# Gated recurrence and four experts on one core: row sums, loads and copies of the attention units moved, and the newer form of unit begun one unit earlier

## The chip, the cores and the metric

The kernel runs on one core of a Trainium2 chip, as one launch. The metric is the device time of the run in microseconds (us). The core's engines are PE (matrix products), DVE, ACT and POOL (elementwise work), and SP, which here only issues DMAs; PE's weight loads are shown apart as PEld. Each engine works through its own queue in order and waits on semaphores that other engines or DMAs raise.

## What is computed

The first part is a gated linear recurrence over 768 steps for 4 batches of 8 heads with 48 columns; the second sends its output through four small two-layer networks ("experts") and adds their results with normalised weights.

```python
# q, k, v, alpha: (4, 8, 768, 48)
for t in range(S):
    state = alpha[:, :, t, :, None] * state + np.einsum('bhd,bhe->bhde', k[:, :, t], v[:, :, t])
    y[:, :, t] = np.einsum('bhd,bhde->bhe', q[:, :, t], state)
x = y.transpose(0, 2, 1, 3).reshape(B * S, H * D)            # (3072, 384)
...
p = domain_probs / (domain_probs.sum(-1, keepdims=True) + 1e-09)
for e in range(E):                                           # E = 4, w1 384 x 1024, w2 1024 x 384
    h = np.maximum(x @ w1[e], 0.0)
    out += p[:, e:e + 1] * (h @ w2[e])
```

## The kernel before

**Units.** The sequence is cut into 6 chunks of 128 tokens (`cb`); one chunk of one batch `b` is a unit, so there are 24 units (0 to 23), dealt chunk by chunk. They form groups of 2, 4, 4, 4, 4, 4 and 2 units. A unit's result is a slice of `xT`, the input of the experts for its group. The attention of a group runs beneath the experts' work of the group before it; in the start-up the first two units run alone and beneath the first expert.

**The experts.** `up(gi, e, fc)` (L962) makes one of 8 slices of a hidden layer: after group 0 nine matmuls of 128x512 into a PSUM tile `one` (three products of high and low parts, L995), ACT's relu into the high part of `hT` (L1003), and later, one slice behind, DVE's low part (`hidden_rest`, L1035), which reads `one` again and so gives the PSUM buffer back. `one` and the sums `ops` of `down` (L1038, matmuls L1083) share four PSUM buffers, tag "g". `add_up` (L1107 and L1109) weights the sums. Weights are split once into high and low parts (L261 to L264, `kept`) and later loaded from there (`w<-kept`, L234).

**A unit in the older form** is `attention(u)` (L718). It turns alpha, k and q into columns (PE transposes `tp`, L295, or DVE for units from `in_runs` = 6 on), then doubles the span of tokens that a block covers in seven levels (m = 1, 2, 4 to 64). Level `li` has a copy of query halves into a tile `qb` (`copy_q`, L781, two copies of 64 partitions on ACT), `next_q` (L788 on DVE and the decay product L790 on POOL) and `next_k` (a copy of key halves, L799, and L800 on DVE). The decay tile `AT` is multiplied in place, so each level's query and key products read what POOL's product of the level before wrote. Levels 0 to 5 give score products on PE (`sc`, L807), of which DVE takes the wanted parts into `near` (L817); level 6 gives `far` (L863). After that come the copies into `lat`, the output products `yps` (L902), the keys turned by PE (`tp`, four transposes, copied by ACT at L735 for alpha and in `turn_keys` for keys), the state products `sps`, and the state update (L941). `sps` and `tp` share the PSUM tag "w" with two buffers.

**A unit in the newer form** is `in_order(u)` (L497), taken from `in_fours` = 8 on. Levels 0 and 1 are replaced by products of four neighbouring tokens: q is loaded by fours into two large tiles (eight DMAs, L183) and three shifted rows of alpha into `ra` (L186); POOL multiplies them (L517 twice, then L520 and L521 for each tile), DVE sums the rows into `dot` (L531), and a later step writes those sums into `near`. The two levels still advance queries, keys and decays, but have no copies into `qb`, no score products and no takes. Levels 2 to 6 stay (`copy_q` L551, `next_q` L557 and L559, `next_k` L568 and L571, score products L604). The keys are turned through DRAM: DVE transposes blocks into a tile that POOL stores in `over` (L644), and four DMAs of SP load them back over `AT` (`AT<-over`, L656) for the state products (L696). These units run two at a time, overlapped: the tail of unit u-1 runs inside unit u.

**The order.** Each unit is a generator, and each `yield` ends a step. `deal()` (L1129) gives every step a time on a clock that `advance()` (L1185) moves by the estimated cost of each slice of experts' work; when the clock passes a step's time, the step's instructions are put into the queues of their engines, behind what is there. The tables `BEATS`, `HEAD_EARLY`, `HEAD`, `HEAD_FIRST`, `HEAD_SECOND` and `REST` (L137 to L142) hold the times as shares of a unit; `HEAD_FIRST` and `HEAD_SECOND` are those of the first two units of the newer form. The second unit is `attention(1)`, whose steps are set by hand in the start-up. `load(u, names)` (L155) issues a unit's loads on SP; it is called from steps of the unit before, and the loads of q by fours write the tiles that the unit before sums up, so they come behind its row sums. `load(u + 2, "v")` is in an older unit's last step. Large tiles for the newer form are popped one after the other out of twelve tiles (`raws`) that hold unsplit weights in the beginning.

Of the kernel before, what the change touches and what calls it, by code (L numbers as in the profile page):

```python
# [16 lines left out]
AX = mybir.AxisListType  # L17
# [3 lines left out]
def kernel(  # L21
# [11 lines left out]
    nc = tc.nc  # L33

    B, H, S, D = q.shape
# [5 lines left out]
    QUAD = 32  # L41
# [13 lines left out]
    n = np.arange(QUAD)[None, :]  # L55
# [4 lines left out]
    t = np.arange(HALF)[None, :]  # L60
# [30 lines left out]
    half = B // 2  # L91
# [10 lines left out]
    NTOK = P // QUAD  # L102
# [5 lines left out]
    fours = {}  # L108
# [32 lines left out]
    HEAD_SECOND = [0.02, 0.06, 0.1, 0.13, 0.16, 0.2, 0.25, 0.31, 0.37, 0.45, 0.52, 0.61, 0.66]  # L141
    REST = [0.05, 0.17, 0.3, 0.42, 0.58]  # L142
    in_runs = half + B
    in_fours = half + 2 * B - 2
    MARGIN = 6.0
    waiting = deque()
    clock = 0.0
# [7 lines left out]
    def load(u, names):  # L155
        if u >= len(units):
            return
        cb, b = units[u]
        for nm in names:
            src = srcs[nm][b, :, cb * P:(cb + 1) * P, :].rearrange("h s d -> s h d")  # L160
            if u == in_fours and nm == "q":
                nc.gpsimd.memset(row_a, 1.0)
            if u == in_runs and nm != "v":
                nc.gpsimd.memset(runs_of[nm][:, :, RUN - HD // 4:], 0.0)
            for g in range(P // QUAD if u >= in_runs and nm != "v" else 0):
                i, tail = divmod(g, 2)
                off, n = (QUAD, RUN - HD // 4) if tail else (0, RUN)
                runs = srcs[nm][b].rearrange("(a i) s d -> i a (s d)", i=2)[
                    i, :, cb * P * D:(cb + 1) * P * D].rearrange("a (t n) -> t a n", t=QUAD)
                nc.sync.dma_start(out=runs_of[nm][QUAD * g:QUAD * (g + 1), :, :n],  # L170
                                  in_=runs[:, :, off:off + n])
            if u >= in_runs and nm == "a":
                continue
            if u < in_fours or nm != "q":
                nc.sync.dma_start(out=raw(u, nm)[:, :, :D], in_=src)  # L175
                continue
            by_four = lambda t: t[b, :, cb * P:(cb + 1) * P].rearrange("h (t f) d -> t h (f d)", f=FOUR)
            if u == in_fours:
                four_tiles.extend(whole_raw(keep=True).rearrange("p (h f d) -> p h f d", f=FOUR, d=D) for _ in range(2))
            fours[u] = four_tiles  # L180
            for i, t in enumerate(fours[u]):
                for j in range(FOUR):
                    nc.sync.dma_start(out=t[j::FOUR].rearrange("p h f d -> p h (f d)"),  # L183
                                      in_=by_four(q)[:, H // 2 * i:H // 2 * (i + 1)])
            for j in range(FOUR - 1):
                nc.sync.dma_start(out=row_a[j::FOUR].rearrange("p h f d -> p h (f d)")[:, :, D * j:],  # L186
                                  in_=by_four(alpha)[:, :, D * (j + 1):])
# [309 lines left out]
    def in_order(u):  # L497
        cb, b = units[u]
        k = u - in_fours
        keep = cb < NCB - 1  # L500
# [6 lines left out]
        AT, QT = AT_of[k % 3], QT_of[k % 3]  # L507
# [10 lines left out]
        for i, t in enumerate(fours[u]):  # L518
            some = slice(H // 2 * i, H // 2 * (i + 1))
# [6 lines left out]
        turn("k", KT)  # L526
        yield
        dots = hid.tile([P, H, FOUR], F32, name="dot", bufs=1)
        for i, t in enumerate(fours.pop(u)):
            some = slice(H // 2 * i, H // 2 * (i + 1))  # L530
            nc.vector.reduce_sum(out=dots[:, some], in_=t, axis=AX.X)  # L531
            yield
        load(u + 1, "k")
        turn("q", QT)
        nc.vector.tensor_mul(QT, QT, AT)
        yield
        load(u + 1, "q")

        decs = [AT]
        KTs = [KT]  # L540
# [33 lines left out]
        for li in range(2):  # L574
            next_q(li)
            next_k(li)
            yield
        if k == 0:
            fifth = whole_raw(keep=True)[:, :NP * P].rearrange("p (a i n) -> p a i n", i=2, n=HALF)
            nc.gpsimd.memset(fifth, 0.0)  # L580
            free.append(fifth)
# [54 lines left out]
        if keep:  # L636
            next_k(6)
            if not quads:
# [3 lines left out]
                                in_=KTs[-1].rearrange("x a (t n) -> x a t n", n=QUAD))  # L642
            over = dram.tile([P, NTOK, NP * QUAD], F32, name="over", bufs=2)
            nc.gpsimd.dma_start(out=over, in_=by_quad.rearrange("x t a c -> x t (a c)"))  # L644
        yield
        parts = lat.rearrange("p (r s i) c -> p r s i c", s=2, i=2)
        for s in range(2):
            rows = slice(HALF * s, HALF * (s + 1))
# [3 lines left out]
            rows = slice(HALF * s, HALF * (s + 1))  # L652
            nc.scalar.copy(out=lat[rows, :, rows], in_=near[rows])
        yield
        for t in range(NTOK if keep else 0):
            nc.sync.dma_start(out=AT[QUAD * t:QUAD * (t + 1)],  # L656
                              in_=over.rearrange("(g r) t n -> t r g n", r=QUAD)[t])

        st = sts[b]
        flat_st = st.rearrange("p a i d -> p a (i d)")  # L660
# [57 lines left out]
    def attention(u):  # L718
        cb, b = units[u]
# [27 lines left out]

        own = rk[:, :, :D]
        own_late = u == 1
        copy_k = nc.gpsimd.tensor_copy if u == 1 else nc.scalar.copy  # L750
        if not own_late:
            nc.gpsimd.tensor_mul(own, rq[:, :, :D], own)
        yield
# [20 lines left out]
        def copy_q(li):  # L774
            m = LEVELS[li]
            qv = halves(QT, m)[:, :, :, 1, :]
            qb = free.popleft()
            qbs[li] = qb
            for i in range(2):
                rows = slice(HD * i, HD * (i + 1))  # L780
                nc.scalar.copy(out=qb[rows, :, i, :].rearrange("p a (b r) -> p a b r", r=m),  # L781
                               in_=qv[rows])

        def next_q(li):
            m = LEVELS[li]
# [7 lines left out]
        def next_k(li):  # L793
            m = LEVELS[li]
            old = new = halves(KTs[li], m)
            if li + 1 < len(LEVELS):
                KTs.append(keys())
                new = halves(KTs[-1], m)
                copy_k(out=new[:, :, :, 1, :], in_=old[:, :, :, 1, :])  # L799
            nc.vector.tensor_mul(new[:, :, :, 0, :], old[:, :, :, 0, :],  # L800
                                 spread(halved(decs[li])[:, :, :, 1], m))

# [326 lines left out]
    def deal():  # L1129

        wanted = [0.0]
        ends = [0.0, 0.0]
        events = []
        times = []
        t = 0.0
        for (gi, e), after in zip(tasks, tasks[1:]):
            part = 1 - 1 / len(groups[0]) if gi == e == 0 else 1
            t += (cost(0, gi, e) * FCH + cost(1, gi, e) * len(groups[gi])) * part  # L1140
            if after[1] == 0:
                wanted.append(t)

        for gis in [*([gi] for gi in range(1, LAST - 1)), [LAST - 1, LAST]]:
            gi, due = gis[0], wanted[gis[-1]] - MARGIN
            n = sum(len(groups[i]) for i in gis)
            first = wanted[gi - 1] - MARGIN * (2 < gi < LAST - 1) if gi > 1 else 0.0
            space = (due - first) / (n if gi > 1 else (n + 1) / 2)
            if gi == 1:
                space /= 2  # L1150
            for k in range(n):
                u = sum(map(len, groups[:gi])) + k
                end = due - (n - 1 - k) * space
                begin = max(end - 2 * space, ends[-2])
                ends.append(end)
                if u >= in_fours:
                    run = in_order(u)
                    burst, lead = ends[-2], ends[-2] - ends[-3]
                    span = end - burst
                    if u < in_fours + 2:  # L1160
                        times.append([burst - lead * (1 - f) for f in (HEAD_FIRST, HEAD_SECOND)[u - in_fours]])
                    else:
                        times.append([ends[-3] - (ends[-3] - ends[-4]) * (1 - f) for f in HEAD_EARLY])
                        times[-1] += [burst - lead * (1 - f) for f in HEAD]
                    times[-1] += [burst] + [burst + span * f for f in REST] + [end] * (u == len(units) - 1)
                    events += [(time, u, run) for time in times[-1]]
                    continue
                run = attention(u)
                beats = [0.0, *BEATS]
                due_at = {-1: begin, **{j: begin + (end - begin) * beats[j + 1] for j in (7, 11, 16)}}  # L1170

                marks = sorted(due_at)
                times.append([])
                for lo, hi in zip(marks, marks[1:]):
                    times[-1] += [due_at[hi] if j == hi else
                                  due_at[lo] + (due_at[hi] - due_at[lo]) * (beats[j + 1] - beats[lo + 1])
                                  / (beats[hi + 1] - beats[lo + 1]) for j in range(lo + 1, hi + 1)]

                for j, ahead in ((6, 13), (12, 15)):
                    if times[:-1]:  # L1180
                        times[-1][j] = max(times[-1][j], times[-2][ahead] + 0.5)
                events += [(time, u, run) for time in times[-1]]
        return sorted(events, key=lambda x: x[:2])

# [88 lines left out]
```

## Time and profile before

| | |
|---|---|
| median of 3 runs | 962.15 us (961.38 to 962.58) |
| the profiled execution | 961.24 us |
| its span (first to last instruction) | 959.5 us |
| busy time of PE, DVE, ACT, POOL | 948.1, 523.8, 376.4, 283.1 us |
| granted TensorE clock | 1.0 |
| DMA moved | 188.09 MB, mean 196 GB/s |
| largest groups on PE: L1083 / L995 | 376.0 us (x2112) / 361.4 us (x1656) |

The busy time of an engine is the time in which it had an instruction at work; the rest of the span is idle time, and the profile names for each idle stretch the instruction or DMA that ended it. In rows of the timeline the columns are the start and the length in us, the engine, the line and operation, the tiles written and read, the shape, how many records the row holds, and in brackets the idle time before it and its releaser. A row of L807 or L604 counts two records for a product. Lines are those of the kernel before; in the changed kernel most stand one to six lines higher or lower.

### The profile page before, as it was taken

What the parts mean: (1) busy time and instruction counts of PE and PEld (TensorE: products, weight loads), DVE (VectorE), ACT (ScalarE), POOL (GpSimd) and SP (SyncE); (2) the same over time, 40 slices, a digit from 0 to 9 for tenths busy, and PEclk for the clock granted to TensorE, in tenths of its full rate; (3) what the DMA queues carried; (4) which work ended last, traced back from release to release, by engine and by line L of the source; (5) the groups of instructions that cost most, each with busy time, mean ns of one, the idle gap of its engine ahead of it and who ended that gap; (6) DMA issues with size and microseconds to landing.
All of it is one profiled execution on the core that took longest, in us unless ns stands there. A gap on an engine that the chain in (4) does not pass through costs nothing.

```text
span 959.5 us, 21105 instructions
## 1 busy us (share of the span) xinstructions
PE 948.1 (99%) x8456; PEld 854.2 (89%) x8456; DVE 523.8 (55%) x971; ACT 376.4 (39%) x819; POOL 283.1 (30%) x397
## 2 busy tenths in 40 slices
PE   9999999999999999999999999999999999999998
PEld 7788778898998988989989989889899899999997
DVE  5667767577666665755646647647674312221222
ACT  5687756445154243242441441544234212021111
POOL 3332332444453441542533425424441000000000
PEclk9999999999999999999999999999999999999999
DMA  7999758697866687746686864678870006070701
GB/s 175 281 327 283 234 149 260 230 345 239 279 222 203 179 301 250 207 169 177 188 287 205 269 204 126 196 252 216 272 229 25 20 4 260 1 264 1 262 18 33
DMA packets 171270, 188.09 MB, mean 196 GB/s; under 512 B 83436, under 2 KB 151404, under 8 KB 171172
## 3 DMA queue, kind: packets, MB, share of 16 engines
q1 hardware_dynamic: 163748, 153.74, 53.2%
q0 software_dynamic: 6976, 32.64, 8.8%
q8 instruction: 67, 1.10, 0.5%
q10 hardware_dynamic: 448, 0.36, 0.2%
q14 instruction: 31, 0.25, 0.1%
HBM read 153.67 MB, written 33.03 MB: 195 GB/s over the span
## 4 chain that ended last, share of the span: by engine, by line
PE 87%; DMA 4%; ACT 2%; SPq 2%; DVE 2%; issue 1%; POOL 0%; DVEq 0%; ACTq 0%; POOLq 0%
PE ops L1083 39%; PE one L995 38%; PE sc L604 3%; PE yps L677 3%; PE sc L807 2%; DMA raw<-in_moe_w_dram 2%; DMA AT<-over 1%; DMA kept<-w 1%; ACT qb L781 1%; PE tp L295 1%; PE yps L902 1%; SPq L183 1%; PE sps L614 1%; PE sps L696 0%; SPq L175 0%
## 5 line engine op out<-in xcount | busy, mean ns | idle before, releaser
L1083 PE MATMUL ops<-w,hT 128*128 128x384 f32 x2112 | 376.0, 337 | 0.7 <-DVE hT L1035 0.6
L1083 PEld LDWEIGHTS ops<-w,hT 128*128 128x128 f32 x2112 | 365.6, 188 | 5.5 <-issue 2.4
L995 PE MATMUL one<-xT,w 128*128 128x512 f32 (+1 forms) x1656 | 361.4, 377 | 0.0
L995 PEld LDWEIGHTS one<-xT,w 128*128 128x128 f32 x1656 | 296.5, 188 | 57.1 <-issue 0.3
L1003 ACT ACTIVATE hT<-one 128x512 fp32r<-128x512 f32 (+3 forms) x232 | 120.6, 524 | 317.8 <-PE one L995 315.8
L1035 DVE SCALAR_TENSOR_TENSOR hT<-one,hT 128x512 fp32r<-128x512 f32 (+1 forms) x192 | 120.2, 640 | 105.8 <-ACT hT L1003 105.8
L559 POOL TENSOR_TENSOR AT<-AT 128x256 f32<-128x256 f32 (+2 forms) x66 | 30.6, 464 | 178.1 <-DVE QT L557 178.0
L1109 DVE SCALAR_TENSOR_TENSOR acc<-ops,p_all,acc 128x384 f32<-128x384 f32 x66 | 38.7, 611 | 76.9 <-PE ops L1083 76.9
L557 DVE TENSOR_TENSOR QT<-QT,AT 128x256 f32<-128x256 f32 x77 | 37.4, 485 | 69.4 <-ACT qb L551 51.2
L1118 POOL DMA_DIRECT2D out_dram<-acc x22 | 11.8, 542 | 199.1 <-DVE acc L1109 199.1
L521 POOL TENSOR_TENSOR raw<-raw,rk 128x768 f32<-128x768 f32 x32 | 60.3, 1883 | 2.5
L520 POOL TENSOR_TENSOR raw<-raw,ra 128x576 f32<-128x576 f32 x32 | 50.9, 1591 | 1.3
L781 ACT COPY qb<-QT 64x256 f32<-64x256 f32 x98 | 40.2, 410 | 16.6 <-DVE QT L788 12.3
L1083 PE MATMUL ops<-raw,hT 128*128 128x384 f32 x128 | 45.6, 494 | 0.4 <-ACT hT L1003 0.4
L551 ACT COPY qb<-QT 64x256 f32<-64x256 f32 x88 | 35.3, 401 | 16.3 <-DVE QT L557 12.5
L531 DVE TENSOR_REDUCE dot<-raw 128x16 f32<-128x768 f32 x32 | 29.7, 931 | 19.8 <-POOL raw L521 19.8
L559 POOL TENSOR_TENSOR raw<-raw 128x256 f32<-128x256 f32 (+5 forms) x30 | 14.0, 466 | 86.8 <-DVE raw L557 86.8
L264 POOL DMA_DIRECT2D kept<-w x32 | 18.6, 582 | 68.7 <-DVE w L263 33.3
L686 ACT CAST xT<-yps 128x384 fp32r<-128x384 f32 x14 | 6.7, 479 | 74.5 <-PE yps L677 74.5
L790 POOL TENSOR_TENSOR AT<-AT 128x256 f32<-128x256 f32 (+5 forms) x42 | 19.4, 462 | 55.1 <-DVE QT L788 54.9
L995 PE MATMUL one<-raw,w 128*128 128x256 f32 x288 | 35.2, 283 | 0.0
L995 PEld LDWEIGHTS one<-raw,w 128*128 128x128 f32 x288 | 35.1, 192 | 0.0
(171 smaller groups left out, 981.6 us busy)
## 6 DMA issues: line engine op xcount, KB each, us to landing
w<-kept SPq DMA_DIRECT2D x108, 768.0 KB, 6.0
kept<-w POOLq DMA_DIRECT2D x32, 768.0 KB, 5.7
raw<-in_moe_w_dram SPq DMA_DIRECT2D x44, 384.0 KB, 7.1
raw<-in_q_dram SPq DMA_DIRECT2D x128, 96.0 KB, 2.8
rv<-in_v_dram SPq DMA_DIRECT2D x24, 192.0 KB, 3.8
out_dram<-acc POOLq DMA_DIRECT2D x22, 192.0 KB, 2.8
rk<-in_k_dram SPq DMA_DIRECT2D x18, 192.0 KB, 3.1
sa<-in_alpha_dram SPq DMA_DIRECT2D x36, 88.0 KB, 2.8
```

Source lines behind the costliest of these rows:

```text
L520: nc.gpsimd.tensor_mul(t[:, :, 1:], t[:, :, 1:], row_a[:, some])
L521: nc.gpsimd.tensor_mul(t, t, row_k[:, some].unsqueeze(2).broadcast_to([P, H // 2, FOUR, D]))
L531: nc.vector.reduce_sum(out=dots[:, some], in_=t, axis=AX.X)
L551: nc.scalar.copy(out=qbs[li][rows, :, i, :].rearrange("p a (b r) -> p a b r", r=m), in_=qv[rows])
L557: nc.vector.tensor_mul(qv, qv, spread(dv[:, :, :, 0], m))
L559: nc.gpsimd.tensor_mul(dec, dv[:, :, :, 0], dv[:, :, :, 1])
L781: nc.scalar.copy(out=qb[rows, :, i, :].rearrange("p a (b r) -> p a b r", r=m), in_=qv[rows])
L995: nc.tensor.matmul(one, lhsT=w[:, of_w, kc], rhs=x_part(gi, of_x)[:, kc, :n], start=k == 0, stop=k == len(turns) - 1)
L1003: nc.scalar.activation(out=parts[0], in_=one, func=ACT.Relu)
L1035: nc.vector.scalar_tensor_tensor(out=low, in0=x, scalar=0.0, in1=top.bitcast(F32), op0=ALU.max, op1=ALU.subtract)
L1083: nc.tensor.matmul(sums[slot], lhsT=h, rhs=w, start=(n == begins[slot]), stop=(n == ends[slot]))
L1109: nc.vector.scalar_tensor_tensor(out=acc, in0=part, scalar=scale, in1=acc, op0=ALU.mult, op1=ALU.add)
```

## The change

1. `in_fours` is one less, 7: the eighth unit (unit 7, the second of group 2) takes the newer form, so that 17 units have it in place of 16; `HEAD_FIRST` and `HEAD_SECOND` are those of units 7 and 8 now.
2. In the newer form the two row sums come after levels 0 and 1 and not before the turn of q; `load(u + 1, "k")` comes two steps sooner and `load(u + 1, "q")`, which has to be behind the sums, later.
3. The loads `AT<-over` are issued one yield behind the store into `over`, two steps sooner than before.
4. In the second unit ACT takes the copies of key halves from POOL, and DVE takes the second of the two query copies of each level from ACT.
5. In the older form the last step (state update and load of a later v) is put one unit of the clock after the step before it.

```diff
-    in_fours = half + 2 * B - 2
+    in_fours = half + 2 * B - 3
...
         dots = hid.tile([P, H, FOUR], F32, name="dot", bufs=1)
-        for i, t in enumerate(fours.pop(u)):
-            some = slice(H // 2 * i, H // 2 * (i + 1))
-            nc.vector.reduce_sum(out=dots[:, some], in_=t, axis=AX.X)
-            yield
         load(u + 1, "k")
         turn("q", QT)
         nc.vector.tensor_mul(QT, QT, AT)
         yield
-        load(u + 1, "q")
...
             next_q(li)
             next_k(li)
             yield
+        for i, t in enumerate(fours.pop(u)):
+            nc.vector.reduce_sum(out=dots[:, H // 2 * i:H // 2 * (i + 1)], in_=t, axis=AX.X)
+            yield
+        load(u + 1, "q")
         if k == 0:
...
             nc.gpsimd.dma_start(out=over, in_=by_quad.rearrange("x t a c -> x t (a c)"))
         yield
+        for t in range(NTOK if keep else 0):
+            nc.sync.dma_start(out=AT[QUAD * t:QUAD * (t + 1)],
+                              in_=over.rearrange("(g r) t n -> t r g n", r=QUAD)[t])
         parts = lat.rearrange("p (r s i) c -> p r s i c", s=2, i=2)
...
             nc.scalar.copy(out=lat[rows, :, rows], in_=near[rows])
         yield
-        for t in range(NTOK if keep else 0):
-            nc.sync.dma_start(out=AT[QUAD * t:QUAD * (t + 1)],
-                              in_=over.rearrange("(g r) t n -> t r g n", r=QUAD)[t])
...
         own_late = u == 1
-        copy_k = nc.gpsimd.tensor_copy if u == 1 else nc.scalar.copy
...
-                nc.scalar.copy(out=qb[rows, :, i, :].rearrange("p a (b r) -> p a b r", r=m),
-                               in_=qv[rows])
+                copy = nc.vector.tensor_copy if u == i == 1 else nc.scalar.copy
+                copy(out=qb[rows, :, i, :].rearrange("p a (b r) -> p a b r", r=m), in_=qv[rows])
...
-                copy_k(out=new[:, :, :, 1, :], in_=old[:, :, :, 1, :])
+                nc.scalar.copy(out=new[:, :, :, 1, :], in_=old[:, :, :, 1, :])
...
                 for j, ahead in ((6, 13), (12, 15)):
                     if times[:-1]:
                         times[-1][j] = max(times[-1][j], times[-2][ahead] + 0.5)
+                times[-1][16] = times[-1][15] + 1.0
                 events += [(time, u, run) for time in times[-1]]
```

## The prediction, made before the changed kernel ran

> **What bounds the kernel now.** I read the table of engines first, then the list of what PE waited for, then the rows in order of time around each wait. The first says which engine sets the time:
>
> ```profile
> PE 948.1 (99%) x8456; PEld 854.2 (89%) x8456; DVE 523.8 (55%) x971; ACT 376.4 (39%) x819; POOL 283.1 (30%) x397
> ```
>
> PE is busy for 948.1 of 959.5 us. So only two things can shorten the kernel: less work on PE, or less of the 11.4 us in which PE stands. Time on DVE, ACT or POOL counts only where PE ends up waiting for it. PE's waits (us in total, times, longest) are few and single:
>
> ```profile
> PE tp L295 <- ACT AT L735: 1.4, 2, 0.7
> PE far L863 <- ACT qb L781: 1.1, 1, 1.1
> PE sps L696 <- DMA AT<-over: 0.8, 1, 0.8
> PE ops L1083 <- DVE hT L1035: 0.6, 1, 0.6
> ```
>
> They lie at 77 and 97 us (tp), 30 us (far), 252 us (sps) and 199 us (ops). After some 260 us PE has no gap but the tail of about 5 us behind its last product. All the change can win is thus ahead of 260 us, apart from work taken off PE. The profiled execution took 961.24 us with a span of 959.5; the median of the runs is 962.15, 0.9 above it. I sum against 961.24 and add 0.9.
>
> **Part 1, the eighth unit (unit 7) in the newer form.** The older form makes levels 0 and 1 by score products on PE. The row of unit 6, `sc<-qb,KT` x64, is four levels:
>
> ```profile
> 141.79 2.08 PE L807 MATMUL sc<-qb,KT 128*64 128x64 f32 x64
> 143.81 12.54 PE L995 MATMUL one<-xT,w 128*128 128x512 f32 x54
> ```
>
> Two levels are half of it, 1.04 us. Its key turn (four transposes, a row of 0.60 us whose last record overlaps the next product by about 0.27) is some 0.33 us and goes too, since the newer form turns keys through DRAM. Far scores, state products and outputs stay. That is **-1.4 us**, the surest term, since PE is full at that place.
>
> In exchange POOL gets the four-token products, which in unit 8 (the first of the newer form before) took 8.9 us:
>
> ```profile
> 176.53 2.11 POOL L517 TENSOR_TENSOR ra<-ra 128x384 f32<-128x384 f32 x2
> 178.72 1.43 POOL L520 TENSOR_TENSOR raw<-raw,ra 128x576 f32<-128x576 f32 x1
> 180.22 1.84 POOL L521 TENSOR_TENSOR raw<-raw,rk 128x768 f32<-128x768 f32 x1
> ```
>
> (L520 and L521 come twice: 2.11 + 2 x 1.43 + 1.84 + 1.92 = 8.7 and gaps.) SP gets eight loads of q by fours and three of alpha in place of one load of 192 KB. DVE swaps a pair of takes (1.5 us) for two row sums of 0.93.
>
> In the changed kernel's order on POOL these products stand behind unit 6's 128x128 decay product and **ahead of its 128x64 one**, which before ran at once:
>
> ```profile
> 133.71 0.48 POOL L790 TENSOR_TENSOR AT<-AT 128x128 f32<-128x128 f32 x1 [3.24 <-DVE QT L788]
> 135.03 0.55 POOL L790 TENSOR_TENSOR AT<-AT 128x64 f32<-128x64 f32 x1 [0.84 <-DVE QT L788]
> 142.19 0.42 DVE L788 TENSOR_TENSOR QT<-QT,AT 128x256 f32<-128x256 f32 x1
> ```
>
> And the products must wait for loads that SP issues only behind unit 7's `sq`:
>
> ```profile
> 127.40 2.00 SPq L170 DMA_DIRECT2D sq<-in_q_dram  x4
> 158.89 6.51 SPq L183 DMA_DIRECT2D raw<-in_q_dram  x8
> 165.50 1.91 SPq L186 DMA_DIRECT2D ra<-in_alpha_dram  x3
> ```
>
> From 129.4: eight issues take 5.2 to 7.5 in the six units of the newer form that I read (mean 6.1), three issues 1.9 to 2.9 (mean 2.3), landing 2.7 behind the last issue's start, so 2.0 behind its end (an issue is some 0.7): the products begin at 129.4 + 6.1 + 2.3 + 2.0 = 139.8 and end 8.9 later, at P = 148.7. Behind P: the 128x64 product (0.55); on DVE, whose queue keeps order, unit 6's third-level QT and KT multiplications (0.75), two takes (1.5), and only then the low part of fc 1 (L1035, 0.68) that gives back a PSUM buffer. Tag "g" has four, so fc 5 of up(1,0) starts at P + 3.45. In the same way fc 6 waits for fc 2's low part (P + 6.4) and fc 7 for fc 3's, behind a split (0.95) and a row sum (0.93): P + 8.9. Before, fc 7 began at 154.2 (143.81 plus five of 2.08). The stall is P + 8.9 - 154.2 = P - 145.3, **+3.4 us**. This is a wait that the trace of before doesn't have. Its ends: shortest issues and products (5.16 + 1.91, then 8.5 with the shortest record of each kind) give P = 147.0 and 1.7 us; longest (7.45 + 2.85, then 10.85 with the longest records, 1.34, 1.90 and 2.18) give P = 152.5 and 7.2 us. I take the means, which most rows are near to.
>
> The spread of the product rows is one DVE operation wide (L520 1420/1436/1901 ns least, median, most, against 0.42 us for a DVE multiplication). [...]
>
> **Part 2, row sums and loads moved within the newer form.** In the newer form the sums wait for POOL's products (L531: 19.8 us of DVE's idle time), and turn q, QT and loads queue behind them. With the sums behind levels 0 and 1, DVE waits at level 1 instead, where the 128x256 decay product stands behind the same products on POOL: the idle time moves, it doesn't go. From 260 us on PE stands for none of it, so zero; if a low part of hT were held up by one row sum more than the PSUM buffers cover, it would cost that sum, 0.93. `load(u+1,"q")` comes later; it fills the same two raw tiles and has most of a period (37.7 us) to land. The ops wait at 199 us (DVE late by one low part, in unit 8's levels) goes, as unit 8 is now the second unit of the form and its levels are dealt by another table (HEAD_SECOND): **-0.6**, 0 at the worst.
>
> **Part 3, AT<-over sooner.** One sps wait came from it:
>
> ```profile
> 238.73 2.76 SPq L656 DMA_DIRECT2D AT<-over  x4
> 251.62 0.55 PE L696 MATMUL sps<-rv,AT 128*32 128x48 f32 x32 [0.76 <-DMA AT<-over]
> ```
>
> Issued two steps sooner, it precedes the three `w<-kept` it stood behind: **-0.8**. But SP now waits at the load until `over` has landed (median 4.0 us), and what is queued behind it, unit 9's sq, eight q and three alpha loads, waits too. Unit 9's products would end near 219, one step ahead of where DVE needs them for the second pair of ops (224): I put **+0.4**, from 0 to 3 with a landing of 11.7, the longest.
>
> **Part 4, the last step of the older units sooner.** At 77 and 97 us the state update stands behind the takes and the next key transposes find their PSUM buffer not yet copied:
>
> ```profile
> 76.68 0.71 DVE L941 COPY st<-sps 64x192 f32<-64x192 f32 x2
> 76.88 0.58 ACT L735 COPY AT<-tp 128x512 f32<-128x512 f32 x1
> 77.51 0.44 PE L295 MATMUL tp<-ident,sk 128*128 128x128 f32 x2 [0.71 <-ACT AT L735]
> ```
>
> Two buffers of tag "w" serve sps and tp. With the update ahead of level 4, sps gives its buffer back some 1.5 us sooner and the key transposes take that one: 0.71 + 0.70, **-1.4**. If the ring hands them the other buffer, 0.
>
> **Part 5, second unit's copies.** far at 30.3 waits for two ACT copies:
>
> ```profile
> 29.40 0.83 ACT L781 COPY qb<-QT 64x256 f32<-64x256 f32 x2 [0.95 <-DVE KT L800]
> 30.33 0.66 PE L863 MATMUL far<-qb,KT 128*64 128x128 f32 x8 [1.09 <-ACT qb L781]
> ```
>
> One of the two (0.41) goes to DVE, which does such a copy in 0.29 (L448), but DVE was busy from 27.09 to 29.33 without a gap; ACT also gets POOL's key copies (0.41). Between -1.1 (whole wait) and +0.3 (one more copy on a full DVE): **-0.45**.
>
> **Sum.** -1.4 - 0.6 - 0.8 - 1.4 - 0.45 = -4.65 of gains; +3.4 + 0.4 of losses; -0.85. 961.24 - 0.85 + 0.9 = **961.3 us**.
>
> **Rivals.** (a) No stall at fc 5 to 7: then -4.65 + 0.4, **957.9**. For it: DVE's and ACT's steps go by the clock of PE's work, so a later emission could leave more room. Against: it needs P under 145.3, products begun by 136.4, while the shortest issues alone last until 136.5. A stall of half the size gives 959.6. Chance of either 0.31.
>
> (b) The slower side, one mechanism: unit 7's products end late, as their loads compete with the weights or DVE stretches them. From P = 151.5 on the loss (6.2 + 0.4) exceeds the gains by 1.95 and the kernel is slower by over 0.2%; at P = 152.5 it is **965.1**. For it: the stretch of 139 to 148.5 has a DMA share of 0.82 before these loads are added, and PE's fc 5 to 7 have only the four buffers. Chance 0.25.
>
> (c) The waits of parts 4 and 5 stay as they are: +1.85, **963.2**, chance 0.09, no difference that shows.
>
> The forecast itself has 0.35. A measurement of this kernel can tell about 0.2% (1.9 us) from no change, so below 960.2 is faster and above 964.1 slower: faster 0.31, same 0.44, slower 0.25. The range reaches from the whole gain with a little more from part 5, 957.3, to P = 152.5 with one more us at unit 9, 966.1.
>
> **What would show it.** In the profile of the changed kernel: `sc` rows of 2.2 us instead of 3.2 in unit 7 and no tp<-KT behind it; no wait at 77 and 97; far's wait near 0.6; no sps wait on `over`. The stall would be PE `one` L993 (was L995) waiting for DVE L1033, three times, 2 to 4 us in all, with POOL's L521 ending near 149. If POOL's products end before 145.3, or PE has no wait between 148 and 160, the main loss is wrong. If the wait is at another unit, the place is wrong.

## The result, and the profile after

The changed kernel takes 965.40 us (median of 8 runs, 963.23 to 967.11), the kernel before 961.72 in the same measurement (8 runs, 961.00 to 962.58). The ratio is 1.0037, 95% interval 1.0028 to 1.0046: slower, by some 3.7 us. The forecast was 961.3, 0.85 below the kernel before and no difference that can be told. The time lies in the range, but on its slower side, which had a chance of 0.25.

The profiled execution took 966.88 us with a span of 965.1. Its table of engines:

```profile
PE 950.0 (98%) x8420; PEld 855.4 (89%) x8420; DVE 538.5 (56%) x978; ACT 371.8 (39%) x811; POOL 291.5 (30%) x397
```

PE has 36 records fewer (32 of score products and 4 transposes, as forecast) and yet 1.9 us more busy time. In the list of what PE waited for (us in total, times, longest), three of the four waits that the change aimed at are gone (tp, sps and ops). The fourth, far's, has grown from 1.1 to 1.8, and two new ones stand ahead of it:

```profile
PE one L993 <- DVE hT L1033: 2.8, 1, 2.8
PE one L993 <- DVE acc L1107: 2.0, 1, 2.0
PE far L861 <- DVE qb L780: 1.8, 1, 1.8
```

That explains longer idle time, not more busy time. The busy time is explained by the clock. Stretches of 5 us behind the three waits, with busy time of each engine, the granted TensorE clock (first number behind POOL's bracket), DMA share and GB/s:

```profile
30.00:35.00 5.00, 3.75 (x42) 2.89 (x42) 3.17 (x10) 2.09 (x5) 0.33 (x1) 0.66 1.30 224
155.00:160.00 5.00, 5.00 (x17) 3.56 (x16) 5.00 (x9) 3.10 (x7) 1.11 (x3) 0.71 0.99 397
230.00:235.00 5.00, 5.00 (x17) 3.93 (x17) 4.07 (x8) 2.03 (x5) 1.61 (x3) 0.70 0.66 174
```

In half-microsecond stretches the clock is 0.50 from 31.6 to 35.0, from 154.5 to 157.9 and from 229.6 to 233.0, and 1.00 elsewhere ahead of the tail: three times about 3.4 us, each losing 1.705 us of clock (half of 3.41). The kernel before kept 1.00 until its last 0.9 us, where PE has no product left; its longest wait was 1.2.

**The wait at 150 us** came as the chain in the prediction had it. Rows of the timeline:

```profile
139.06 2.75 POOL L517 TENSOR_TENSOR ra<-ra 128x384 f32<-128x384 f32 x2 [4.87 <-DMA ra<-in_alpha_dram]
149.42 0.42 POOL L788 TENSOR_TENSOR AT<-AT 128x64 f32<-128x64 f32 x1
149.87 0.42 DVE L786 TENSOR_TENSOR QT<-QT,AT 128x256 f32<-128x256 f32 x1 [2.12 <-POOL AT L788]
153.01 8.21 PE L993 MATMUL one<-xT,w 128*128 128x512 f32 x27 [2.81 <-DVE hT L1033]
```

The products begin at 139.1 (forecast 139.8), take 10.4 us (8.9) and end at 149.4 (148.7); fc 5 starts 3.6 us behind that (3.45). Of the 27 matmuls of fc 5 to 7, 6.24 us at full clock, 8.21 were needed: the half clock, where the prediction had two more waits. fc 7 ends at 161.15, against 156.27 before.

**The wait at 227 us** begins on SP:

```profile
198.85 2.68 SPq L646 DMA_DIRECT2D AT<-over  x4
201.57 2.26 SPq L170 DMA_DIRECT2D sq<-in_q_dram  x4
203.92 6.57 SPq L183 DMA_DIRECT2D raw<-in_q_dram  x8
214.62 2.10 POOL L517 TENSOR_TENSOR ra<-ra 128x384 f32<-128x384 f32 x2 [6.32 <-DMA ra<-in_alpha_dram]
229.08 7.13 PE L993 MATMUL one<-xT,w 128*128 128x512 f32 x23 [1.97 <-DVE acc L1107]
```

From 193.5 to 198.9 SP issued nothing: it stood at `AT<-over` until the store issued at 193.7 had landed (5.0 us by the DMA records; the four loads are issued 5.2 us behind it). With the 2.7 us of these issues themselves, SP lost 8.1 us there. Unit 9's loads of q came behind it, its products ended at 223.4 and not near 219, and DVE's two sums, an xT difference, a state update and two takes stood ahead of the add-up that gives PE its PSUM buffer.

### The profile page after: what moved, and what is told of

It reads as the page before. It is cut to its first block, busy times and chain, and to the rows that moved or that the text cites. A ratio compares the mean times of both kernels' runs of the same rounds, so it can differ in the third digit from the quotient of the medians.

```text
span 965.1 us, 21101 instructions
## 1 busy us (share of the span) xinstructions
PE 950.0 (98%) x8420; PEld 855.4 (89%) x8420; DVE 538.5 (56%) x978; ACT 371.8 (39%) x811; POOL 291.5 (30%) x397
## 4 chain that ended last, share of the span: by engine, by line
PE 90%; DVE 3%; SPq 2%; DMA 1%; issue 1%; POOL 1%; ACT 1%; DVEq 0%; POOLq 0%; ACTq 0%
PE ops L1081 40%; PE one L993 38%; PE sc L603 3%; PE yps L676 3%; PE sc L805 1%; SPq L183 1%; PE tp L295 1%; PE yps L900 1%; PE one L997 1%; DMA raw<-in_moe_w_dram 1%; PE sps L613 1%; DMA sk<-in_k_dram 0%; POOL raw L520 0%; PE sps L695 0%; DVE near L815 0%
## 5 line engine op out<-in xcount | busy, mean ns | idle before, releaser
L993 PE MATMUL one<-xT,w 128*128 128x512 f32 (+1 forms) x1656 | 365.5, 380 | 4.9 <-DVE hT L1033 2.8
L552 DVE TENSOR_TENSOR QT<-QT,AT 128x256 f32<-128x256 f32 x84 | 44.1, 525 | 79.7 <-ACT qb L546 47.3
L554 POOL TENSOR_TENSOR AT<-AT 128x256 f32<-128x256 f32 (+2 forms) x72 | 33.5, 465 | 172.2 <-DVE QT L552 167.8
L521 POOL TENSOR_TENSOR raw<-raw,rk 128x768 f32<-128x768 f32 x34 | 65.5, 1926 | 2.7
L520 POOL TENSOR_TENSOR raw<-raw,ra 128x576 f32<-128x576 f32 x34 | 54.8, 1610 | 1.3
L546 ACT COPY qb<-QT 64x256 f32<-64x256 f32 x96 | 38.5, 401 | 8.5 <-DVE QT L552 4.4
L517 POOL TENSOR_TENSOR ra<-ra 128x384 f32<-128x384 f32 x34 | 35.5, 1045 | 16.9 <-DMA ra<-in_alpha_dram 15.5
L552 DVE TENSOR_TENSOR raw<-raw,raw 128x256 f32<-128x256 f32 x35 | 18.2, 521 | 38.9 <-ACT qb L546 19.7
L566 DVE TENSOR_TENSOR KT<-KT,AT 128x256 f32<-128x256 f32 x81 | 39.3, 485 | 0.0
L780 ACT COPY qb<-QT 64x256 f32<-64x256 f32 x77 | 31.5, 410 | 19.9 <-DVE QT L786 18.1
```

What stands on the lines that cost most here:

```text
L517: nc.gpsimd.tensor_mul(row_a[:, :, j], row_a[:, :, j - 1], row_a[:, :, j])
L520: nc.gpsimd.tensor_mul(t[:, :, 1:], t[:, :, 1:], row_a[:, some])
L521: nc.gpsimd.tensor_mul(t, t, row_k[:, some].unsqueeze(2).broadcast_to([P, H // 2, FOUR, D]))
L546: nc.scalar.copy(out=qbs[li][rows, :, i, :].rearrange("p a (b r) -> p a b r", r=m), in_=qv[rows])
L552: nc.vector.tensor_mul(qv, qv, spread(dv[:, :, :, 0], m))
L554: nc.gpsimd.tensor_mul(dec, dv[:, :, :, 0], dv[:, :, :, 1])
```

## The experiments

Parts are numbered here, and in the expectations, as in the list of the change: 4 is the second unit's copies, 5 the older units' last step (the prediction has these two the other way round). Times are medians; each ratio is against runs of the kernel before on the same chip. The kernel before differs by up to 0.45 us between the chips, so "below" and "above before" go by the runs of the same row; against the changed kernel, each is first set against its own kernel before.

| kernel | us | before | ratio (95%) |
|---|---|---|---|
| part 4 undone | 965.73 | 961.32 | 1.0038 (1.0023 to 1.0053) |
| eighth unit older | 960.19 | 961.32 | 0.9987 (0.9978 to 0.9996) |
| products later | 962.78 | 961.32 | 1.0014 (1.0003 to 1.0024) |
| AT<-over later | 961.78 | 961.32 | 1.0001 (0.9991 to 1.0011) |
| loads by fours early | 963.07 | 961.40 | 1.0016 (1.0005 to 1.0027) |
| all three mended | 959.10 | 961.40 | 0.9978 (0.9969 to 0.9987) |
| eighth older, part 4 undone | 959.91 | 961.40 | 0.9986 (0.9976 to 0.9996) |
| all mended, levels later | 957.61 | 961.27 | 0.9963 (0.9950 to 0.9977) |
| part 5 alone | 960.25 | 961.38 | 0.9985 (0.9977 to 0.9994) |
| parts 3 and 5 alone | 959.29 | 961.38 | 0.9972 (0.9961 to 0.9982) |

### The eighth unit in the older form

```diff
-    in_fours = half + 2 * B - 3
+    in_fours = half + 2 * B - 2
```

> The changed kernel with the eighth unit in the older form again, all other parts as they are. Theory A (the waits of the eighth unit's products and of the third unit of the newer form, with their half clock, are the loss): the wait of 2.8 us at 150 and its 1.6 us of clock go, PE gets 1.4 us of score products and transposes back, so 3.0 us less than the changed kernel, 0.6 above before; if the wait at 227 goes too (2.0 + 1.6), 3.0 below before. Rival B (part 2, the later row sums, makes the wait at 227, whichever unit is the first of the newer form): a wait of about 2 us on a second or third unit's add-up near 265 us, with half clock behind it. Rival C (what is lost comes from the start-up alone): no change against the changed kernel but +1.4.

960.19, 1.1 below before and so 4.8 below the changed kernel (3.7 + 1.1): both waits went, and the half clock with them, that of the start-up too, where far's wait was 1.66 and not 1.84. The third unit of the newer form has no wait on its add-up, so the later row sums are not what makes it (rival B falls). Putting one unit into the newer form costs 4.8 us here, although it takes some 1.4 off PE.

### AT<-over of unit 7 behind unit 9's loads

```diff
+        if k:
+            back()                      # the four AT<-over loads
         parts = lat.rearrange("p (r s i) c -> p r s i c", s=2, i=2)
...
         yield
+        if k == 0:
+            back()
```

> The changed kernel with the four AT<-over loads of unit 7 alone put one step later, behind unit 9's loads of q by fours. Theory A (SP waiting at AT<-over for the store into over until 198.9 us delays unit 9's loads, so its products, so the add-up that PE waits for): unit 9's products begin near 211 instead of 214.6, the wait of 2.0 us at 227 and its half clock go, 3.6 us less than the changed kernel, as fast as before. Rival B (unit 9's loads wait for unit 8's row sums, which end at 198, anyway): products begin at 214 and the wait stays; no change. Rival C: the wait goes, but sps of unit 7 at 216.7 now waits for AT<-over by 1 to 3 us.

961.78, 0.5 above before and so 3.2 less than the changed kernel; theory A had 3.6. Part of it may be the start-up, which this run leaves as it was: in its trace far waits 0.90 and not 1.84, without half clock. SP issues unit 9's sq at 191.6 and the products run from 206.3 to 216.2, 8 us sooner. Neither an add-up nor sps waits.

### The second unit's copies as before

```diff
-                copy = nc.vector.tensor_copy if u == i == 1 else nc.scalar.copy
-                copy(out=qb[rows, :, i, :].rearrange("p a (b r) -> p a b r", r=m), in_=qv[rows])
+                nc.scalar.copy(out=qb[rows, :, i, :].rearrange("p a (b r) -> p a b r", r=m),
+                               in_=qv[rows])
...
-                nc.scalar.copy(out=new[:, :, :, 1, :], in_=old[:, :, :, 1, :])
+                copy_k(out=new[:, :, :, 1, :], in_=old[:, :, :, 1, :])
```

> The changed kernel with part 4 undone: the second unit's copies are those of before. Theory A (a wait of PE near 2 us also halves the granted clock for about 3.3 us behind it, so it costs about 1.6 us more than its length): far's wait falls from 1.84 to about 1.1 us, the clock stays whole between 31 and 35 us, and the time falls by 0.75 + 1.6 = 2.4 us, to 1.2 us above the kernel before instead of 3.6. Rival B (the lower clock belongs to the run and not to the wait): only 0.75 us are won, 2.9 above before, and a stretch at half clock stays near 31 us.

A miss in the time: 965.73. The waits do as expected, 1.09 for far and full clock behind it, but the next load becomes late, and behind 152 us this execution has two half-clock stretches in a row. Two rows of it:

```profile
30.68 0.66 PE L862 MATMUL far<-qb,KT 128*64 128x128 f32 x8 [1.09 <-ACT qb L780]
78.05 0.63 PE L295 MATMUL tp<-ident,sk 128*128 128x128 f32 x4 [1.09 <-DMA sk<-in_k_dram]
```

At this place the changed kernel has no wait for `sk`; why the load comes later here is not shown. Six runs with a mean clock of 0.9965 (the changed kernel's eight: also 0.9965) can't tell whether part 4 alone costs time.

> The changed kernel with the eighth unit in the older form and the second unit's copies as before, so parts 2, 3 and 5 alone. Theory A: far's wait of 1.7 us of the run with the eighth unit older falls to 1.1 and no half clock can follow it: 0.6 to 1.0 less than that run, 1.7 to 2.1 below before. Rival B (part 4 does nothing to the time): the same time as that run, 1.1 below before.

With both undone the far wait is 1.10 instead of 1.66 and the time 959.91 against 960.19; the intervals overlap. What part 4 costs in time where nothing drops the clock can't be told from this. The wait itself is not a fixed size: in the five traces that have part 4's copies far waits 0.90, 1.55, 1.66, 1.84 and 1.84, in the others 0.74 to 1.10.

### Unit 7's products later on POOL

```diff
+            if k == 0 and li == 1:
+                by_fours(0)             # L517, and L520 and L521 of the first tile
...
+            elif i == 0:
+                by_fours(1)             # the second tile
```

> The changed kernel with unit 7's four-token products put into POOL's queue behind unit 6's 128x64 and 128x32 decay products, in two halves around its 128x16 product, and unit 7's two row sums behind its levels 3 and 4. Theory A: the wait of 2.8 us at fc 5 goes, and the half clock with it: 4.4 us less than the changed kernel, 0.8 below before; no PE wait over 1 us between 140 and 165. Rival B (the products take so much of POOL and, by the row sums, of DVE that the wait only moves): a wait of 1.5 us or more between 150 and 170, and a gain under 1.5 us.

In this kernel the products multiply by unit 8's row of k, which is loaded ahead of them, so that part of unit 7's output differs; the work is of the same kind and size. 962.78: the wait at fc 5 went, and a new one of 2.3 us came at unit 6's far scores, with half clock from 158 to 162 (rival B). The rows show why:

```profile
154.03 2.23 DVE L806 TENSOR_TENSOR QT<-QT,AT 128x256 f32<-128x256 f32 x1 [1.36 <-POOL AT L808]
154.53 1.44 POOL L521 TENSOR_TENSOR raw<-raw,ra 128x576 f32<-128x576 f32 x1
156.05 1.88 POOL L522 TENSOR_TENSOR raw<-raw,rk 128x768 f32<-128x768 f32 x1
156.19 2.02 DVE L818 TENSOR_TENSOR KT<-KT,AT 128x256 f32<-128x256 f32 x1
158.35 1.12 PE L881 MATMUL far<-qb,KT 128*64 128x128 f32 x8 [2.30 <-DVE KT L818]
```

DVE multiplications of 0.42 us take 2.2 and 2.0 while a product runs on POOL. POOL's two rows are at their usual length here. The trace of before had it too, where I looked only at POOL's side (ten query multiplications of this shape beside such products took 1.04 there in the median):

```profile
183.67 2.08 DVE L800 TENSOR_TENSOR KT<-KT,AT 128x256 f32<-128x256 f32 x1
```

### Unit 7's loads by fours one step sooner, products behind unit 6's 128x64

```diff
+        if u + 1 == in_fours:
+            load_fours(u + 1)           # memset of ra, L183 x8, L186 x3, ahead of load k and q
         yield
...
-    HEAD_FIRST = [*(0.06 * j for j in range(1, 8)), 0.5, 0.58, 0.66, 0.74, 0.82, 0.93]
+    HEAD_FIRST = [0.11, *(0.06 * j for j in range(2, 8)), 0.5, 0.58, 0.66, 0.74, 0.82, 0.93]
```

> The changed kernel with unit 7's eight loads of q by fours and three of alpha issued before its loads of k and q (one step of unit 6 sooner), and its products put behind unit 6's 128x64 decay product in POOL's queue (HEAD_FIRST begins with 0.11). Theory A (the loss at 150 us is the late loads with the products ahead of the 128x64 product): products begin near 136 and end near 145, no wait at fc 5, no half clock near 155: 2.8 + 1.7 x about 0.9 = 4.3 less than the changed kernel, 0.7 below before. Rival B (the products slow DVE's two-input operations while they run, whatever their place, so low parts come late anyway): DVE's multiplications of 0.42 us take 1 to 2 us beside them and a wait of over 1 us stays between 145 and 160.

963.07, 1.7 above before: half of the expected gain. At 150 us PE waits 1.09 and 0.61 and not 2.81, without half clock there; far (1.55, half clock behind it) and the add-up (1.70, none behind it) are left as they were.

> All three mended at once: unit 7's loads and products as in the run before, its AT<-over loads one step later, the second unit's copies as in the kernel before. Theory A (the three waits and the clock behind them are the whole loss): no PE wait over 1.3 us behind the start-up, clock 1.0 until the tail, and what remains is the gain: score products and transposes 1.4, the two waits at 77 and 97 us 1.4, waits at 199 and 252 us 1.4: 4.2 below before, near 957.3. Rival B: another wait takes the place of one of them, and the gain stays under 2 us.

959.10, 2.3 below before. The clock is whole until the tail; the waits of 1.1 and 0.6 at 149 and 152 are all that is left of the new waits, and about the 1.8 us that are missing from the expected 957.3.

### The same, with unit 7's early levels later on DVE

```diff
-    HEAD_FIRST = [0.11, *(0.06 * j for j in range(2, 8)), 0.5, 0.58, 0.66, 0.74, 0.82, 0.93]
+    HEAD_FIRST = [0.11, 0.12, 0.267, 0.34, 0.415, 0.43, 0.465, 0.5, 0.58, 0.66, 0.74, 0.82, 0.93]
```

> The run with all three mended, and unit 7's turn of q, its levels 0 and 1 and its row sums put later on the clock (HEAD_FIRST 0.267 to 0.465 in place of 0.18 to 0.42), so that DVE does them behind the low parts of fc 1 and fc 2 and not beside POOL's products. Theory A (what is left of the loss, PE's waits of 1.1 and 0.6 us at 149 and 152, is DVE's two-input operations that take 2 to 3 times as long while POOL's products run, with the low parts behind them): the waits fall under 0.5 us together and the time by 1.2 to 1.7, to about 957.6, 3.7 below before. Rival B (the waits come from POOL's decay products, late behind the four-token products, as in the prediction): the same waits, 959.1.

957.61 (five runs), 3.7 below before, the fastest of all. Its list of PE's waits has nothing over 1.2, and all that it has over 0.4 lies in the start-up, the load's 0.5 at 7 us:

```profile
PE idle L1227 <- POOL st L1206: 1.2, 1, 1.2
PE far L874 <- ACT qb L792: 0.7, 1, 0.7
PE tp L299 <- DMA sk<-in_k_dram: 0.5, 1, 0.5
```

POOL's order is that of the run before and its products end at 144.3 as against 144.1, so rival B falls. What moved is DVE work out of the way of fc 1's and fc 2's low parts, 3 us of it, of which only 0.5 was slowing. So the run shows that DVE's queue made the two waits, and not how much of them was the slowing. Beside the products DVE is slowed as in the run before, but nobody waits for it there now: the two weight differences that took 1.82 us before the change take 4.16 in both runs:

```profile
136.56 4.16 DVE L267 TENSOR_TENSOR w<-raw,w 128x768 fp32r<-128x768 f32 x2
```

### What a wait costs in clock

Into the kernel before, far from the attention's busy start, go repeated computations of one low part, in the second such kernel also of half of one (the values stay the same):

```diff
+            more = HOLD.get((gi, e), 0) if fc == 1 else 0
             while finish:
+                for _ in range(more):
+                    hidden_rest(*finish[0])
                 hidden_rest(*finish.popleft())
```

> The kernel before with DVE's low part of fc 0 computed 8 to 15 times over in twelve of the later slices of the experts, so that PE waits at fc 4 for 0 to about 4 us in places where nothing else is late. Theory A (a wait of PE near 2 us is enough to halve the granted clock, by chance, and from about 3.4 us on always): no stretch below full clock behind waits under 1.2 us, some behind 1.7 to 2.5 us, all behind the longest; each such stretch 3.4 us long at 0.50, 1.7 us lost. Rival B (the half clock comes from something else in the first 240 us of the changed kernel): full clock behind all of them.

> As the run with waits of 0 to 6 us, now with waits of 1.4 to 2.2 us in eleven or twelve places of the later slices. Theory A (the chip judges by windows that run on by themselves, so a wait of this length halves the clock or not by where it falls): some of them, between a fifth and four fifths, have a stretch of 3.4 us at 0.50 behind them, and the share grows with the length. Rival B (a fixed length of about 2.5 us decides, and those of 1.55 to 2.3 us in the start-up and at 227 us were helped by idle moments just before): none of them.

| PE's wait, us | 1.1 or less | 1.56 | 1.82 | 2.28 to 2.30 | 2.55 to 2.56 | 3.0 to 3.3 | 4.0 to 6.2 |
|---|---|---|---|---|---|---|---|
| places | 3 | 3 | 4 | 4 | 3 | 3 | 4 |
| half clock near or behind it | 0 | 0 | 1 | 3 | 3 | 2 | 4 |

Three rows of the first of these kernels and two of the second show the same 36 matmuls (four slices) behind waits:

```profile
496.06 8.45 PE L997 MATMUL one<-xT,w 128*128 128x512 f32 x36 [1.82 <-DVE hT L1040]
536.57 10.08 PE L997 MATMUL one<-xT,w 128*128 128x512 f32 x36 [2.55 <-DVE hT L1040]
579.43 8.46 PE L997 MATMUL one<-xT,w 128*128 128x512 f32 x36 [3.27 <-DVE hT L1040]
```

```profile
497.49 10.10 PE L997 MATMUL one<-xT,w 128*128 128x512 f32 x36 [1.82 <-DVE hT L1043]
580.80 8.45 PE L997 MATMUL one<-xT,w 128*128 128x512 f32 x36 [1.82 <-DVE hT L1043]
```

The price is all or nothing: 1.63 us or none, for the same wait of 1.82, and none behind one of 3.27. Every stretch loses 1.7 us or a multiple (3.4 behind 4.72, 5.1 around the one of 6.16 at 667). In these 24 places length sets the odds and not the outcome; rival B of both runs falls.

What else goes with it can be read from the traces. In every trace with more than one of them the half-clock stretches begin whole multiples of 3.413 us apart: in the changed kernel at 31.59, 154.47 and 229.56, which is 36 and 22 of them. Carried on, these marks cut the whole execution into windows of 3.413 us, and what goes with the loss is the time in which PE stands within one window. The wait of 3.27 at 579 is split by a mark into 1.61 and 1.66; the wait of 1.82 at 497 lies in one window whole, and half clock follows it. In these rows the first number behind the length is PE's busy time:

```profile
574.36:577.77 3.41, 1.80 (x8) 1.15 (x7) 3.27 (x5) 0.74 (x2) 0.00 (x0) 1.00 0.98 361
577.77:581.18 3.41, 1.75 (x8) 1.45 (x9) 3.32 (x8) 1.40 (x4) 0.42 (x2) 1.00 0.04 8
495.53:498.94 3.41, 1.59 (x7) 1.23 (x7) 3.32 (x7) 1.10 (x3) 0.42 (x1) 1.00 1.02 404
```

Of the windows at full clock in these two kernels' later slices, none of the 10 with 1.0 to 1.66 us of standing PE has half clock behind it, one of the two with 1.82, and all 12 with 1.99 to 3.41. The three of the changed kernel have 1.84, 1.96 and 1.97. This sorting was made after the runs, and no run was built to test it; one window of 1.55 in a start-up (the run with the loads by fours early) was followed by half clock all the same.

### Parts 5 and 3 by themselves

```diff
                         times[-1][j] = max(times[-1][j], times[-2][ahead] + 0.5)
+                times[-1][16] = times[-1][15] + 1.0
```

> The kernel before with part 5 alone (item 5 of the change: the older units' last step one unit of the clock behind the step before it). Theory A (the prediction's 1.4 us): the two waits at 77 and 97 us go, nothing else appears, 1.4 below before. Rival B (what PE gains there it gives back before 260 us, at the waits at 199 or 252): the two waits go but the time stays within 0.5 of before.

960.25, 1.1 below before: the waits at 77 and 97 go (one of 0.24 on `sk` is left at 76), and 0.3 is given back at the ops wait of 198, now 0.96.

> The kernel before with parts 3 and 5 of the change (AT<-over sooner, the last step sooner) and the row sums where they were. Theory A (the row sums' place is worth nothing): the wait for AT<-over at 252 goes as well, 2.2 below before, that is the same as or a little below the run with parts 2, 3 and 5 (1.5 below). Rival B (the row sums' new place is what gives those parts their room): SP at AT<-over holds back the next unit's loads, a wait on sums or an add-up appears, and the time is 1 us or more above that run.

959.29, 2.1 below before, where 2.2 was expected; the run with the row sums moved as well was 1.5 below, with overlapping intervals. So the place of the row sums is worth nothing that shows.

## Why the prediction was right, and where it failed

Right, with its numbers: the score products and transposes taken off PE (36 records); parts 3 and 5 (2.2 forecast, 2.1 measured by themselves); the row sums as neutral; the chain at 150 us, with its place and the wait at fc 5; the kind of wait at unit 9. The end of the products within 0.7 us is partly luck: they took 1.5 us more than the 8.9 forecast, and their loads landed 0.7 us sooner. The chance of 0.25 for a slower kernel was given for products that end late, at 151.5 or more; they did not, and the kernel was slower for the reasons below.

Wrong (no difference was forecast, and the kernel is 3.7 us slower):

1. **A wait was priced at its length.** The prediction took the clock as full, since the trace of before shows 1.00 everywhere; but that kernel has no wait over 1.2 us, so it could not show what a longer one does. This is the step that failed most. The long waits are now 1.8, 2.0 and 2.8 us, and each had, in the profiled execution, 1.7 us of half clock behind it. Over the eight runs the mean clock was 0.9965, so an estimated two such stretches in a run (3.4 us by 1.7); that also spreads the runs over 3.9 us where those of before spread over 1.6. Behind the wait of 1.84 us and one of four of 1.82 the clock fell to 0.50 for 3.41 us, from one of the marks 3.413 us apart on, and behind one of 3.27 it didn't: some 1.8 us within one window can be enough (1.84, and one of the two windows with 1.82). Why the clock falls is not shown.
2. **SP held at AT<-over: +0.4 was taken, 2.0 came.** The mechanism and its end of the range (3) were there. Mis-sized was what the held SP costs: the store took 5.0 us to land and not the median of 4.0, SP lost 8.1 us with the issues, unit 9's products ended at 223.4 and not near 219, and DVE had more than the sums ahead of the add-up. With the four loads put behind unit 9's loads of q by fours the wait went. (The 11.7 at the upper end was misread: it is the longest of all DMAs of `over`; the stores alone have 7.4 at most in the trace of before.)
3. **The second unit's copies: -0.45 taken, +0.75 came** (1.84 against 1.09), outside the bounds of -1.1 to +0.3. Each level put one more copy on a DVE that was full (four rows of 0.29 to 0.40 from 24.4 us on), and the bound counted only the last of them. The size is that of one pair of traces; others with these copies have 0.90 to 1.84.
4. **DVE's rows beside POOL's products were not read.** I judged by POOL's rows in unit 8, which keep their median, and not by DVE's, which went from 0.42 to 2.08 in the same trace; the sum has no term for it, and only rival (b) names it. In unit 7 of the changed kernel both sides are longer where they run side by side: the products took 10.4 us and not 8.9, and DVE's two weight differences (L263) took 2.64 and a query and a key multiplication (L552, L566) 1.47 and 1.66 (in the trace of before two such differences took 1.82, and a multiplication 0.42). P came only 0.7 us later than forecast (149.4), since the loads came sooner. By the chain behind P the wait at fc 5 would have been shorter with products of 8.9; by how much no run shows.

The sum: forecast -0.85, measured +3.7, 4.5 apart. Unit 9's wait gives 1.6 (2.0 - 0.4), the copies 1.2 (0.75 + 0.45), the stall at 150 us -0.6 (2.8 in place of 3.4); the 2.3 left are put down to the clock, by difference. The mean clock of 0.9965 over 965 us is 3.4, part of it in the tail and in time in which PE stood anyway. The two profiled executions, 5.6 us apart, show where it came, stage by stage. By the time of the kernel before, the experts' products begin 2.5 us later at 38 us, level at 100 (the waits of part 5 gone), 4.9 later at 154 (fc 5: 2.8 and 2.0 of clock), 2.5 at 219 (less work on PE and no ops wait: 2.4 where 2.0 was forecast), 6.3 at 229 (the add-up: 2.0 and 1.7 of clock), and 5.0 from 258 on (no sps wait). Part 4's own price in time stays open.

## What to carry to other kernels

PE is busy for 98% of the span here, and one new wait of 2.0 us came with 1.7 of half clock, 3.7 in all, while one of 3.27 had none behind it, by where it fell. So keep each under about 1.2 (no trace here has half clock behind a shorter one), and read the granted clock behind every wait before adding up their lengths. When work goes to an engine that has time to spare, look at what is queued behind it there (POOL's decay product), what is queued behind its loads (SP), and whose operations it slows while it runs (DVE): here the kernel with any one of three waits mended was no faster than before (965.73, 961.78, 963.07), and with all three it was 2.3 us faster. Pairs were not run. An early issue of a load that must wait for a store isn't early for the queue: SP stood at it for 5.4 us.

## What was not expected of the hardware

A half-clock stretch ahead of the tail has a fixed length in these traces, 3.41 us, or is two or three of them (6.83 us behind the wait of 4.72 in the first kernel with repeated low parts, and behind one of 2.81 in the run with part 4 undone; 10.24 around the one of 6.16). DVE's 128x256 multiplications `QT<-QT,AT` and `KT<-KT,AT` took 0.5 to 2.1 us beside POOL's four-token products in the two traces of before and after, and 2.2 and 2.0 with the products later, in place of 0.42, while transposes and row sums on DVE kept 1.1 and 0.9 beside them.
